# Reading the parts of a filter spectrum backwards in every second batch, under a new table of the order

## The chip, the cores and the metric

The kernel runs on one core of a Trainium2 chip. The metric is the device time of one execution in microseconds (us). Before the change three timed runs gave 484.12 us in the median (484.09 to 484.51). About 0.2%, that is 1 us, is what a measurement of this kernel can tell from no change.

## The reference

Two layers follow one another on four batches of 6272 positions with 256 channels. The first is a gated recurrence along the positions, the second a long convolution with a gate:

```python
f = lower_bound + (1 - lower_bound) * sigmoid(f_logit)      # (4, 6272, 256)
h = f[:, t] * h + (1 - f[:, t]) * x[:, t]                    # for t in 0..6271; y[:, t] = h
x1, x2, x3 = split(y @ w_proj)                               # three times 256 columns
conv = irfft(rfft(x2, axis=1) * rfft(filter_fft, axis=0))    # over all 6272 positions
out  = (x1 * conv * x3) @ w_out                              # float32
```

The spectrum of `filter_fft` doesn't depend on the batch. The kernel computes it once.

## The kernel before

**Stages.** `prepare` makes the tables and the filter's spectrum and writes the spectrum to device memory in 16 parts, `H[0]` to `H[15]` (NU = 16 units). Then each batch b goes through these steps, and the steps of neighbouring batches are interleaved:

- `hgrn(b)`: 13 chunks of 512 positions. Each loads 512 KB of `f_logit` (tile FL) and 512 KB of `x` (tile XT) from three buffers in turn, takes the sigmoid on ScalarE (L311), multiplies on GpSimd (L313), transposes on TensorE (`su`, L325), forms the gate (`f`, L338 on ScalarE or L340 on VectorE) and runs the recurrence as a scan on VectorE (L346).
- `spectrum(b)`: `phase_p` (13 groups `P`, TensorE L673, each evacuated by a copy `x2`), which needs every scan of the batch. Then, for each of four quarters, four `phase_f1` (TensorE L686, copies `A`), a small product `mini`, and four `unit`s. A unit loads its part of the spectrum into one of three slots of the tile `Hu` (NH = 3; line L721, 98 partitions of 4 KB, 392 KB in one DMA), does a transform `F2` (TensorE L731), two products with `Hu` on VectorE (`prod`, L744), and an inverse transform `I2` (TensorE L754) with its copy `Th`.
- `gate(b)`: the products of the two other projections (TensorE L373, copies `xs`, GpSimd L389).
- `phase_o(b)`: 13 groups: inverse transform `I1` (TensorE L787), product `y` on VectorE (L793), output projection `proj` (TensorE L805), a copy `o` into one of three buffers `osb` (ScalarE or VectorE, L272 and L277), and a store of 512 KB (L815). Group k's copy uses buffer k mod 3 (within batch 0), so it waits for the store of group k - 3.

**Slots.** The slot of unit u of batch b is `(16 b + u) mod 3`, and all 16 parts are loaded in each batch: 64 loads of 392 KB. A load waits until the products of the unit that had the slot before are done.

**The order.** Nothing is scheduled by a program on the chip. Every step is recorded with `op(kind, cost, fn, ...)`. `Plan.emit` then issues the steps in the order of the table `ORDER`, a string that was worked out offline. An entry of it names a step, the engine that does it and the pair of PSUM banks. Copies may be done by ScalarE or VectorE, and the table decides. Each engine works through its own entries strictly in order, and all DMAs of the kernel are issued by SyncE's one queue (SP), in order too: a DMA that waits for its buffer holds up the DMAs behind it.

In this text `o0.9` is the copy of group 9 of batch 0, `store0.6` its store, `FL3.6` the load of chunk 6 of batch 3 into FL, `P1.4` group 4 of `P` of batch 1, and `H1[u 2]` the load of the spectrum's part 2 for batch 1. A turn is the stretch around the `P` groups, where one batch gives way to the next. SP's order at the turns before the change (the steps that matter):

```
turn 0 to 1:  store0.5 FL2.1 H1[u 2] store0.6 store0.7 XT2.2 FL2.2 XT2.0 store0.8 H1[u 1] H1[u 0] H1[u 3] store0.9 H1[u 4] H1[u 5]
turn 1 to 2:  XT2.7 H2[u 1] FL2.8 ... FL3.0 H2[u 2] XT3.0 store1.7 FL3.1 FL3.2 store1.8 H2[u 0] XT3.2 H2[u 3] FL3.3 H2[u 4]
middle of 2:  store1.11 store1.10 H2[u 14] H2[u 15] XT3.6 FL3.6 H3[u 0] FL3.7 XT3.7 store1.12
turn 2 to 3:  store2.2 H3[u 1] FL3.12 store2.3 store2.5 store2.4 XT3.12 ... store2.10 H3[u 2] H3[u 3] H3[u 4] store2.8 store2.9 H3[u 5]
```

Of the kernel before, what the change touches and what calls it, by code (L numbers as in the profile page):

```python
# [25 lines left out]
TB = 98  # L26
# [32 lines left out]
class Plan:  # L59
# [58 lines left out]
    "A8gAAYBBgAOYABIAoQBLgACIBGgAmRBVgBQgAcSBagBfgAnTA7YAPIAyUBkgA9AAlVBpgBCAA+WBugBDQBAGAjSA/GBMYA6TBFABzgAgUBHY"  # L118
    "A5VBEIAQABNWERgA2SBPOA1TARIAvUBWAAYYB4gBIQAsVBRABXSADgAtUBOGBSUBYCAfWBbYESgBKAAxXArWBJABgYAeXBZCEdgBcQA3WBlA"
    "BTMBhSEpgApXBdIBqYBUEBmWATIBjCEegAUIBoGBvYBrUBeIBtEBiKAzQAFgBnGB0YBwQBsMAiSByABxIEqgB1WASAAGgAwTB5YETAB3OB9Y"  # L120
    "B6UA0SB2OAbQB7MAkRB8MCKSCIWAEYEUYCLCCBQEfACJOB/UAWICCICNSCAECEWCOKEVQCFGEgYEZUEWIAdSErAE1gAqTEXIE2gAhWEaECTS"
    "AIAAVYEbMEhWAHACDYElQAJAEsYEiOCUCCRUFBgEmAFCgEjOClSCSECQgCGgANACWUEnIE3ACMYEtWCVYCXEEuOExQE4YEvOFNgCmCCcUFOg"
    "EyACZgCaSCdMFDACjWEzIE5UCbCCkGE9SCeYE6MFEYALACfQFZgE+CE7MAuWFagAMACsWCPgAKACHgCgICuUCtGFPAFFWE/KFJQFGGFQYFjg"
    "CvEFHOCoSFkgFKAC3UChgCYgFbACpKA4WCnYFRWC4EFLIFcYCxSFSGFVUCyCFTOC1QFtgFugFWEC+SCqgEwYC2AFdWFXMCrgFlAE0YC6QCwY"
    "C5YC/CDAUC7IFmYFeGFgSDBEFfODJQFhCF3gC9gDHUDKAF4gFiKAXYFnWFvACigEcYDDQDCYFoODIEFqSFwYDEADSUFpOGBgGCgFrCDQQCzg"
    "DTEDMWC0gFsKDRADFgFMYFxUF5AC8gE8YDbQDNODLYFyEDZSDUYFAYDcADGgDVWFzMF6YDaCF0QDWGDiSF1IGLgDkUGMgDjKGDADeWEYYF2I"
    "DtSDlEDdYDYgGEYDfGDrUDOgF7QDsEDnWDuCF8IF+UDoGF9IEoYD0SGVgDmYF/EFYYD2WDqgDPgD1CDwQAaYGAMGWgD3GD/SDpgGNADxIGFW"
    "DhgDvYD5UGOYGGGEAKGIQD6EGHOD9SMVgGJADXgEIUD8gD+CEGWD4YGKIFIYEJEGPSEkYEHGGSUGXAGQKEBYECQEKYGTEMhgGYYGRKEPWD7g"
    "EDAAZYMWgMigGUMEQGGZSELQFUYGfgEFgGaCGcWJSUEEgGbKB+YGdGMXAJTVGeOJUMGgSEMAJVNGmWJWYGhCEOgDygGiUMtgMjAMugGsQDgg"
    "GnGGqSGtIDzgG0WGrCGwQHEgGjEENgGoSG1GGyUGpCGuWGzMGxAG2SGvGGkQG3KMvAG4UJXWGlAG5MJYXJcSJZGJdTJaHHLgG6QJfLG8UHSg"  # L130
    "JbYG7AJeKG+WJhTG9MG/GJgYHFQJiSJjDHHIHAWJkCJmUHBGHIIJlYJnVHMSJoEHCWJrQHPKHZgJpFJsRJtAJqYHiUJuBHOKJwQJxTJvYJyA"
    "J1RHDOHqgHjEJ2SJzLJ6QHGYJ3BHgWJ4KJ0YHJUHhGHTRHUYHKEHNYHkWJ5YHVJJ7TJ8AJ/UHlGHWJHQQJ9DHaVHRAKBMHxgJ+YHrSHcNKAX"
    "HmQHbYKCHMwYHdNHXUHnAKEXHYEHuKHeQH4gKGHIGUKDYHtKHfAHoWKFTIHEHyQHpOH/gKJSKHDH0IHsYIIUKLCKIYHvWIJEH1IH5SHzYHwG"
    "IKUH6YMYYH7KIQgH2QILEIAWH8KH3AIMUKKSINEICOIXgH9QKMCKOTIDOKPUH+AKNYKTVKQDIOQIegIRWKREIPIIBYKUSKVFKSYITOIsTKWC"
    "IEQItDIUOISYIYVIZYKXYIFAKYSIaNIlgKZUKaCKdTIuQIbNKfDKeXIvAIVSKbMI2gIfVKgHKcYIWCImQIiNKiUIcSIgYKkEKhYIhNKjXIdC"
    "KnWIpIKlHIjUI9gKpGKmYI3SIkEIoIIwWInYKoRIxGMkYI5KIqUJEgKqBKsQI6KKtWIrEI+RKvGMZUKrYJLgJAJKuAMdWMaEKxTKwYM5gMeG"
    "MbMKyQM6gKzDK2RK0AJBJIyTK4BK1YIzDMlQMfOK3VMcYMmAMpSK5FMnII0WMqCNFgMxUK6YNGgM7AI1OK7QMrKK8RI/YMyEI4YM1WM8YK+B"
    "MzMK9ANRgI7SM2GNSgLARI8CM3OLBQJGYJFULCBK/YLFSLDAJHMNHAM9WLEYNBQJIMM+GJCTNdgLHCNIYNegM/ONCALGVLKSNTANDIJMWLIF"
    "NUYJDDLLVJOONJQLMCLNFLPTJPONKANNUNfALJYNngNLINVWNogNOELQSLOYLRDNPMNZQNWGNgYRVTLSCNxgNXONaAJJUNygRXDRWSJKENbI"
    "LTYNhWRYCNkTNpANiOJNYJQQN8gNjONlDN7gNqYRaVJRARbSNmLRdCLUWRcFLZQLVONQYNrSNuUNsCLaILWWOFgNzAOGgNtKLbQNvEN0YLXG"  # L140
    "NwMLjSN9ALeWLYgLkKM0YLcAN1UN+YLfOLoSN2ELdgN4QN3MLgWN5AOPgOQgOHAMgYN6ILlULhGOIYLpKLtQLmELigN/WLuIOCSOAGLqUMsY"
    "OZgODCOBONMYOagLngNAYLyQLrEOEKNYYOJWORAOMULsgLzILvSUYgONEOSYOKGOOML0QObALwCOLOL3UMoAOcYLxgOTSM4YL4MOWWOUCL1A"
    "UkgOVKL8UPVgNEAOdQL2gOXGL9ML5SOeANcAOfIL+UL6COYOOgQL/EMGSL7gOhIUxgMBWOiIUwgMLUMCOUZgOvQMAgMHKPOgMDWOwAPHgOpS"
    "MEGOnQOqKOzWOoAO3SO0GOlQO4COtWOmAOrSOuOO5QOsCOxWO6IUyAO1SOyGMMMOjQO2CO7WMIUOkAO8OMNSUmAMJMMQQMOCO9WMRIO/UO+O"
    "RZYPBQPAEPDSPCIPIWReYPECPPUUaAPKOPFQRfSUzYRgTRhCPGIRkWRiDPLOPjQRmGPlSPkAPJYRlWRjYPSMPcgRpXRnGMFgPMQPmCPQYPRM"
    "RoYPWVRrHPdSPYNPtgPNARqUPXYRuXRsEPZNPTQRwHRtYPpUPUAPfKPnWP0gPeYPqEPaQUbYPgKPoGPuURvSP7gPbAPwMRzTUlgPrWRxCPhQ"
    "R1DPsOR0SPxMPvYP1TRyYR2CQJWPiAP4LQCgR4SQKGPyQP3LP8UR6CP9YP2YQLWPzAR3YP+MQTgP5SQMGQDQP/MP6CQNWR5UQGIQOGQagQAS"
    "R7ER9VQFIQUWQBCR8YR+RR/FQWOQhgQPSSABQEYSCUQQCSBYQHQQXOQbVQIAQRSSDXQogQdNSEESHQSFHSIRSJAQSKSGYUcUSKBQeNQvSUdE"
    "SMXQVYQwCQcYUeMQxQSLYQ5gSNWSOHQYSQyISPGQiUQZCSQYQzWQkMSRQQ0GSSRQlMQfSSUBQpWSTAQqYRAgQgCQ1USVYQsOUgQQ2ESWSQjY"
    "QrOU9gUnYUhASXTQmUSZDUiIRHgSYCQtWU8gQnEQ3SQ6QSaYQ4KQuGRBUQ8ISbSRCYScTSdCSgWRDMSeDShXSiGUoSSfYREMSjHSlQUpCSmU"  # L150
    "SkYQ9ISnASqWSoESrXQ7YRIUU+AUqKSpYROgQ+QMPgSsGStPU/YRFSQ/ARLMUsWRGCSvQVIgRKMUtGRPRVJgSxASuYSwVUuOS0TSyFS1QRJY"
    "S2DSzYU0URSJS3AS5WU1ES6XRQYRRJS4YS7GU4SS8HS+QVUgU2MS9YVKARTWVVgS/RRUGU5KRMUVLYTBJTAATDWRNEU6KVAQTEXVBATFOVEU"
    "TCYTGHVCITISVFEVhgVMWVggTHYVWAVGMMKgVQQTJTVNGVqgVXYTKKMSUTLDVOOVRATNSMTETOTTPCMUgTSUVSITMYTQDVYVVrgXRgTTXVZF"
    "TXSTRYTVPTUEVcQVaNViATWYZYXV0gZZUV1gVdAVjYZdVTYKZeWZaHZgGZfNTZSVsAVeITcWTaCTdOThQVtYZbEVkSTbgVnUTiIVlCTeWV+g"
    "VoEV/gVmKVuQTfGVpMTmSV2ATggVxWTnKWJgTjUVvAV3YWIgVyGVwITrSTkEVzOWAATlgV4QV7UV5ATsKWBYToWWSgUjAV8EV6ITtSTpGV9M"
    "T1QUvYTuCTqgTwWVPYWTgUfAT2IWCSTvgU3YVbAWFUU7YWDCTxOT3QWcgWKAWdgWEKTyWWGEWLYWUAWHMT6STzGT7KT/UVTYT4AWMWUAMWPS"
    "WVYWNGT5gT8QWQCT0gWOOUEUT9AWRKVHYWWWWeAVfYWZQWXGUFMWfYUBScogWaAVDYcbgUrAWYOXYgUGUUCCccgT+gWbIWgWWjScngWhGUHE"
    "czgWiOUDgUJQWkKUOWWlKUKIW+UXKgW4SW/EUPOW0Qc0gW5CULUW1AW8WcdAWoSW9OWyQWpCWsWUMEWwSWtOWzAW2UcpAWuQW3EcqYW6WWvA"
    "WmUW7OWxCWqQWnMUQWWrAUTSURGXAUUUKXCQZhYXBMXESXDAXGWZcYXFKXLUXHGXSQceYc1AXOMXISZiWZjXZkGXJKZnVZlHXVIXmSZpFXMY"
    "XoWXnCZmYZoVXNMZsRZqFcfSXTYZuBXUIZrYXfgcjUcgCZtRc/gXpGchKZxQXwgdAgckEZyWZvJcrSZzAclMZ0GXWQcsCZ1YXsWXXActKXgU"  # L160
    "ZwYXZQXtGXjMcvSXhYdBAXPWc2YXiMZ2VcwCXQGXcIZ3UX+gdLgZ4FXqWUIgcxKZ5EZ7RXrGZ8VZ6YaAUXbIaBSZ9BXkWXaYaDCZ+NX3gaCE"
    "XdQdMgXlGZ/YXuSX4UXvKXeAYOWX5YXxSdCYYPGYMQX0Kc3WYNAXzKaFTc4GaEYc7QaHDX6MYFgaGSc8AaKTaICX7MaLUaMDaJYaPSaNEaQT"
    "c9IdNAYWgX8UXyYdYgaOYdXgX9EaSLX1Qc5OaRCdOYX/TX2AaUVYBLaVSaWFYQWaXCYGQYCLaTYYRGYSSaZVYIIYTCYdgaYYaaWaeXabFafU"
    "YJIYHYacGdDSYAYc6YahEYUVajQdECYkgYVNadYakRagHdFKYKUdZAYDWYfYaiYamJalAYXSYEGaoRYZKanYYLEYyWapQYzGYaKYeUYYYatS"
    "arAYgMYbWYrgaqBavCY0QasYYhMYcGYlTauSY1AYmYYoLYiWY8gawCY2QYjGYtYYnLaxYYsUY3AaySYuMY4WZDgdaYa0CYpQUSgY5GUNgYvM"
# [21 lines left out]
def kernel(  # L187
# [102 lines left out]
    def halves(pb, hn):  # L290

        a = PS[:, pb, 0:hn]
        return bass.AP(tensor=a.tensor, offset=a.offset,
                       ap=[a.ap[0], [768, 2], a.ap[1]])

    count = dict(x=0, f=0, s=0, o=0)


    def hgrn(b):
        for c in range(NCHK):  # L300
            t0 = c * CH
            nb = min(CH, S - t0) // 128
# [574 lines left out]
```

## Time and profile before

| | before |
|---|---|
| median of three timed runs | 484.12 us |
| the profiled execution's own time | 487.22 us |
| its span | 485.2 us |
| TensorE (PE) busy, share of the span | 451.7 us, 93% |
| VectorE (DVE) busy | 413.3 us, 85% |
| ScalarE (ACT) busy | 423.0 us, 87% |
| GpSimd (POOL) busy | 299.6 us, 62% |
| moved by DMA | 116.49 MB, 240 GB/s in the mean |
| share of the 16 DMA engines taken by the kernel's queue | 70.0% |

The profiled execution took 2.0 us more than its span, and 3.1 us more than the median of the timed runs. In the rows, a time is that of the profiled execution, counted from the span's start. PE is TensorE's matmuls, PEld its weight loads; SPq is the queue of SyncE. "idle before" with an arrow names the work whose end released the waiting instruction. The chain of waits follows the execution back from its last instruction, always to what came last. Tables by stretch give the busy time of each engine in a stretch with the number of its instructions, then the granted TensorE clock as a share of full speed, the mean busy share of the DMA engines, and GB/s moved.

### The profile page before, as it was taken

To read this page: it belongs to the slowest core of one execution; us is meant where nothing else is said; L and a number is where in the kernel's file an instruction comes from. 1 tells how busy PE (TensorE), PEld (TensorE's weight loads), DVE (VectorE), ACT (ScalarE), POOL (GpSimd) and SP (SyncE) were. 2 spreads that over 40 slices of the span, in tenths; PEclk is the share of its full clock that TensorE was granted. 3 is DMA by queue.
4 is the path that set the end of the run, shared out by engine and by line. 5 is a ranking of instruction groups with operands and counts; after the bars stand their busy time and mean duration, and the time that the engine had idled before them with its cause. 6 is when DMAs were issued, how large, how long until landed. Compare 5 with 4: busy or idle time off the path is not lost.

```text
span 485.2 us, 14710 instructions
## 1 busy us (share of the span) xinstructions
PE 451.7 (93%) x6041; PEld 347.1 (72%) x6041; DVE 413.3 (85%) x446; ACT 423.0 (87%) x613; POOL 299.6 (62%) x313
## 2 busy tenths in 40 slices
PE   8988998999999989999998998989989899999995
PEld 7776777677667879767566888656757788676784
DVE  7788985899999985999999984979989984999773
ACT  6988999999998969989898978999979868999844
POOL 6775994486897910946896723878675522666600
PEclk9999999999999999999999999999999999999998
DMA  8989999545688994464879975475777861544177
GB/s 330 397 287 354 329 306 313 188 122 162 208 274 291 356 346 173 134 195 135 240 236 360 386 265 228 152 232 190 227 245 250 315 227 38 178 148 151 54 287 294
DMA packets 41731, 116.49 MB, mean 240 GB/s; under 512 B 4384, under 2 KB 6304, under 8 KB 41664
## 3 DMA queue, kind: packets, MB, share of 16 engines
q1 hardware_dynamic: 41664, 115.56, 70.0%
q8 instruction: 47, 0.77, 0.7%
q14 instruction: 20, 0.16, 0.1%
HBM read 84.54 MB, written 31.00 MB: 238 GB/s over the span
## 4 chain that ended last, share of the span: by engine, by line
PE 46%; DMA 17%; DVE 14%; ACT 10%; issue 5%; POOL 3%; SPq 1%; ACTq 0%; DVEq 0%; POOLq 0%
PE PS L373 11%; DMA out_dram<-osb 8%; PE PS L673 7%; DMA FL<-in_f_logit_dram 6%; PE PS L754 6%; DVE PP L744 5%; PE PS L805 5%; DVE HA L346 5%; PE PS L731 4%; PE PS L686 4%; PE PS L325 4%; DMA Hu<-H 2%; ACT osb L272 2%; ACT fTs L338 2%; PE PS L787 2%
## 5 line engine op out<-in xcount | busy, mean ns | idle before, releaser
L389 POOL TENSOR_TENSOR zt<-x1s,x3s 128x490 f16<-128x490 f32 (+1 forms) x104 | 125.3, 1214 | 94.5 <-ACT x3s L270 43.9
L744 DVE TENSOR_TENSOR PP<-PS,Hu 98x1008 f16<-98x1008 f32 x128 | 146.5, 1199 | 8.6 <-PE PS L731 3.3
L313 POOL TENSOR_TENSOR XT<-XT,FL 128x1024 f32<-128x1024 f32 (+1 forms) x52 | 116.8, 2247 | 47.5 <-ACT FL L311 18.6
L346 DVE TENSOR_TENSOR_SCAN HA<-fTs,HA,PS 128x512 f16<-128x512 f32 (+1 forms) x96 | 113.4, 1204 | 6.9 <-ACT fTs L338 5.9
L373 PE MATMUL PS<-HA,W 128*128 128x490 f16 (+1 forms) x416 | 105.5, 370 | 3.1 <-DVE PP L744 1.4
L793 DVE TENSOR_TENSOR ys<-PS,zt 128x1024 fp32r<-128x1024 f32 (+1 forms) x52 | 58.6, 1151 | 9.0 <-PE PS L787 3.6
L272 ACT ACTIVATE osb<-PS 128x1024 f32<-128x1024 f32 (+1 forms) x49 | 47.7, 988 | 19.6 <-PE PS L805 11.1
L338 ACT ACTIVATE fTs<-PS,nomc 128x512 f32<-128x512 f32 (+1 forms) x89 | 59.3, 680 | 4.6 <-PE PS L325 4.1
L270 ACT CAST HA<-PS 128x1024 f16<-128x1024 f32 x57 | 57.8, 1032 | 3.8 <-PE PS L686 3.3
L805 PE MATMUL PS<-Wo,ys 128*128 128x256 f32 x392 | 56.8, 291 | 3.2 <-ACT osb L272 1.7
L311 ACT ACTIVATE FL<-FL 128x1024 f32<-128x1024 f32 (+1 forms) x52 | 53.1, 1021 | 7.6 <-DMA FL<-in_f_logit_dram 7.4
L272 ACT ACTIVATE x1s<-PS 128x490 f32<-128x490 f32 (+1 forms) x95 | 56.0, 592 | 3.5 <-PE PS L373 1.3
L373 PEld LDWEIGHTS <-W 128*128 128x128 f16 x416 | 33.9, 98 | 33.7 <-issue 10.8
L754 PEld LDWEIGHTS <-PP 98*128 98x128 f16 x1024 | 49.5, 98 | 11.9 <-issue 3.3
L270 ACT COPY x3s<-PS 128x490 f32<-128x490 f32 (+1 forms) x90 | 51.8, 579 | 4.6 <-PE PS L373 3.1
L805 PEld LDWEIGHTS PS<-Wo,ys 128*128 128x128 f32 x392 | 49.0, 188 | 7.9 <-ACT osb L272 2.2
L325 PE MATMUL PS<-iden,FL 64*128 64x64 f32 x784 | 46.6, 233 | 7.8 <-ACT afs L270 2.1
L754 PE MATMUL PS<-VA,PP 98*128 98x98 f16 x512 | 51.8, 207 | 1.6 <-DVE HA L346 0.9
L270 ACT CAST Th<-PS 128x784 f16<-128x784 f32 x62 | 50.9, 830 | 1.4 <-PE PS L754 1.2
L325 PEld LDWEIGHTS PS<-iden,FL 64*128 64x128 f32 x784 | 34.0, 139 | 25.2 <-DVE HA L346 5.6
L754 PE MATMUL PS<-VB,PP 98*128 98x98 f16 x512 | 51.6, 207 | 0.0
L673 PE MATMUL PS<-W,HA 128*128 128x256 f16 x392 | 44.8, 273 | 3.4 <-ACT osb L272 3.4
(110 smaller groups left out, 677.9 us busy)
## 6 DMA issues: line engine op xcount, KB each, us to landing
Hu<-H SPq DMA_DIRECT2D x64, 392.0 KB
FL<-in_f_logit_dram SPq DMA_DIRECT2D x48, 512.0 KB
XT<-in_x_dram SPq DMA_DIRECT2D x48, 512.0 KB
out_dram<-osb SPq DMA_DIRECT2D x48, 512.0 KB
X<-in_moe_filter_fft_dram SPq DMA_DIRECT2D x9, 512.0 KB
H<-Hu SPq DMA_DIRECT2D x16, 196.0 KB
H<-Hu SPq DMA_DIRECT2D x16, 128.0 KB
Hu<-in_moe_filter_fft_dram SPq DMA_DIRECT2D x2, 512.0 KB
```

The source lines that it names most:

```text
L270: nc.scalar.copy(dst, src)
L272: nc.scalar.activation(dst, src, AF.Copy, scale=scale)
L313: op("u", {"POOL": 0.1 + 0.553 * nb}, lambda e, xt=xt, ft=ft: nc.gpsimd.tensor_tensor(xt, xt, ft, op=AOP.mult), r=[("ft", k)], w=[("xt", k)])
L325: nc.tensor.transpose(bank(pb)[:, at[p] + j:at[p] + hn:nb], src[ps, j, cols], iden[ps, ps])
L338: nc.scalar.activation(fT, sT, AF.Identity, scale=by, bias=1.0)
L346: nc.vector.tensor_tensor_scan(h, fT, bank(pb)[:, 512 - hn:512 + hn], init, op0=AOP.mult, op1=AOP.add),
L373: nc.tensor.matmul(PS[:, p, 0:n], W13[:, kh, js], HA[:, HB[kh] + t0:HB[kh] + t0 + n], start=(kh == 0), stop=(kh == 1))
L389: nc.gpsimd.tensor_tensor(late["zt"][:, jb, :, m0:m0 + nm], xs(0), xs(1), op=AOP.mult),
L673: nc.tensor.matmul(pp[:, r - r0, :], column(HB[kh], q_of(r)), W2[:, kh, :], start=(kh == 0), stop=(kh == 1))
L744: nc.vector.tensor_tensor(PP[:TB, k, o, :, :, 1:64], px.unsqueeze(1).broadcast_to([TB, 2, UE, 63]), hh[:, :, :, 1:64], op=AOP.mult)
L754: nc.tensor.matmul(PS[:, ib + o, pr * TB:(pr + 1) * TB], PP[:TB, k, o, n, 2 * pr:2 * pr + 2, :], v[:TB], start=(n == 0), stop=(n == 1))
L805: nc.tensor.matmul(po[:, i, :], late["ys"][:, yk, kh, i * 128:(i + 1) * 128], Wo[:, kh, :], start=(kh == 0), stop=(kh == 1))
```

## The change

`unit` no longer computes its slot from the batch and the unit. The list `held` says which part lies in each of the three slots, and `recent` orders the slots by their last use. A unit whose part is held takes that slot and issues no load; any other takes the slot that has gone unused longest. In batches 1 and 3 the quarters, and the units in each, are taken from the last to the first. Batch 0 ends on parts 13, 14 and 15, and batch 1 begins with 15, 14, 13; it ends on 2, 1, 0, with which batch 2 begins; and so on. So the first three units of batches 1, 2 and 3 have no load, and 55 of the 64 loads remain.

```diff
+    held, recent = [None] * NH, list(range(NH))
+
+    def spectrum_load(u, h):
+        first = count["h"] < NH
+        count["h"] += 1
+        held[h] = u
+        op("H", {"SP": 0.46}, lambda e: nc.sync.dma_start(
+            Hu[:TB, h].rearrange("p a e k -> p a (e k)"), twice(H[u][:])),
...
     def unit(b, u):
         ka = u % NA * UE
-        k = (b * NU + u) % NP
-        h = (b * NU + u) % NH
-        op("H", {"SP": 0.46}, lambda e: nc.sync.dma_start(
...
+        k = count["u"] % NP
+        count["u"] += 1
+        h = held.index(u) if u in held else recent[0]
+        recent.remove(h)
+        recent.append(h)
+        if held[h] != u:
+            spectrum_load(u, h)
...
     def spectrum(b):
         phase_p(b)
-        for q in range(NU // NA):
-            for u in range(q * NA, q * NA + NA):
+        way = 1 if b % 2 == 0 else -1
+        for q in range(NU // NA)[::way]:
+            for u in range(q * NA, q * NA + NA)[::way]:
                 phase_f1(b, u)
             mini(b, q)
-            for u in range(q * NA, q * NA + NA):
+            for u in range(q * NA, q * NA + NA)[::way]:
                 unit(b, u)
```

The string `ORDER` is replaced as a whole. From the two built programs, engine by engine:

- TensorE has the same 770 steps. Up to a few neighbours that change places they stand in the same order, but for the turns. At turn 0 to 1 the old table has one `P` group, `proj0.9`, then the other twelve; the new one has ten `P` groups, `proj0.9`, two, `I1` 11 and 12, the last. At turn 1 to 2 the old one has `proj1.10` after three `P` groups and `proj1.11` after all, the new one has both after all thirteen.
- 11 more steps are done by VectorE (406 for 395), 7 fewer by ScalarE, 4 fewer by GpSimd. VectorE's part of the copies changes thus: `x2` +4, `afs` +4, `f` +3, `o` +3, `Th` +1, `fr` +1, `f2` -3, `hw` -2. Four of GpSimd's `wrap` copies (L280) go to ScalarE. `o0.9`, `o1.10` and `o2.10`, done by ScalarE before, are done by VectorE at the turns, `o0.9` after ten `P` groups and `o1.10` after all thirteen; `o0.12` goes to VectorE in the middle of batch 1, `o1.12` leaves it.
- SP's order at the same places:

```
turn 0 to 1:  store0.5 FL2.1 XT2.1 store0.6 store0.8 XT2.2 XT2.0 FL2.2 store0.7 H1[u 12] H1[u 11] ... H1[u 5] store0.11 H1[u 4] store0.10 H1[u 3] H1[u 2] H1[u 1] FL2.3 XT2.3 store0.9 H1[u 0]
turn 1 to 2:  XT2.7 XT2.8 ... store1.5 store1.6 store1.7 FL3.0 store1.8 FL3.1 FL3.2 XT3.0 XT3.2 XT3.1 store1.9 H2[u 3] XT3.3 H2[u 4] FL3.3
middle of 2:  store1.10 H2[u 11] ... H2[u 15] FL3.6 store1.11 XT3.6 XT3.7 FL3.7
turn 2 to 3:  store2.2 store2.3 FL3.12 XT3.12 store2.4 store2.5 store2.6 store2.7 store2.10 store2.8 H3[u 12] H3[u 11] ... H3[u 5] store2.9 H3[u 4]
```

- In `prepare`, the loads of `x` for batch 1 (XT1.0, XT1.1) come after the last stores of the spectrum and the first two loads of it, where before they came ahead of them; two fewer of the spectrum's stores stand ahead of XT0.11 (14 for 16).

## The prediction

> **What bounds the kernel now.** I read the page first (busy shares and the DMA row), then the table in stretches of 10 us, then the chain of waits and the order of time at the turns.
>
> ```profile
> PE 451.7 (93%) x6041; PEld 347.1 (72%) x6041; DVE 413.3 (85%) x446; ACT 423.0 (87%) x613; POOL 299.6 (62%) x313
> ...
> DMA  8989999545688994464879975475777861544177
> ...
> Hu<-H SPq DMA_DIRECT2D x64, 392.0 KB
> ```
>
> No engine is the bound throughout. TensorE is idle for 485.2 - 451.7 = 33.5 us, and no more than that, plus a lower clock, can be won at its waits. The DMA row is full in four places: up to 90 us, and around the three turns. There the table shows who pays:
>
> ```profile
> 160.00:170.00 10.00, 10.00 (x162) 8.87 (x158) 10.00 (x10) 9.28 (x13) 8.88 (x8) 1.00 1.01 349
> 170.00:180.00 10.00, 9.37 (x157) 8.33 (x152) 8.95 (x10) 7.22 (x11) 1.49 (x3) 1.00 0.99 331
> 180.00:190.00 10.00, 8.26 (x77) 8.13 (x76) 4.15 (x4) 7.42 (x8) 0.00 (x0) 1.00 0.80 291
> ...
> 290.00:300.00 10.00, 8.35 (x75) 8.13 (x74) 4.50 (x4) 7.96 (x9) 2.40 (x1) 1.00 0.81 320
> ```
>
> The columns after the stretch are PE, PEld, DVE, ACT, POOL, clock, DMA share and GB/s. At 160 to 180 the DMA share is 1.0 at 331 to 349 GB/s, and TensorE's idle time comes directly after. The order of time names the wait:
>
> ```profile
> 171.87 0.65 SPq L721 DMA_DIRECT2D Hu<-H  x1
> 172.72 3.13 SPq L815 DMA_DIRECT2D out_dram<-osb  x2
> ...
> 181.71 1.02 ACT L272 ACTIVATE osb<-PS 128x1024 f32<-128x1024 f32 x1 [2.38 <-DMA out_dram<-osb]
> ```
>
> `store0.6` goes out directly behind a load of the spectrum that nobody needs before 196 us. In the chain of waits it takes 8.89 us to land; ScalarE holds `o0.9` for it, and with it everything behind; the next `P` group waits for that copy's PSUM pair, 1.74 us of TensorE. Turn 1 to 2 repeats it: a load of the spectrum at 283.68, `store1.7` at 284.58, which lands after 9.19 us, `o1.10` at 293.79, TensorE idle for 1.65 us before 294.87.
>
> **The change part by part.** *The nine loads.* Each is 392 KB, that is 0.401 MB, and at the mean of the two rows, 340 GB/s, takes 1.18 us of a full queue: 3.5 us at each turn, 10.6 us in all. [...] But eight of the nine were issued in full stretches (171.87, two from 179.27, 253.75, 283.68, 287.81, 352.84, 378.46; only 398.53 is not), and what they push back are stores and loads that are waited for. So the gain isn't 10.6 us but what TensorE gets back of its waits there:
>
> - (a) Turn 0 to 1: 1.74 us. `store0.6` loses the load ahead of it (1.2 us), and `o0.9` now comes after ten `P` groups on VectorE, some 8 us later (the chain has 8.24 us for 74 of a batch's 98 `P` matmuls, 0.11 us each, and eight in a group), when the store has landed. I take 1.7; ends 0 and 1.7.
> - (b) Turn 1 to 2: the same for `o1.10` and `store1.7`, 1.65 us; the stretch 260 to 280 has 2.0 us more of idle TensorE, scattered over waits for FL, XT and `osb`; one load (253.75) goes from ahead of it. I take 1.6 + 0.4 = 2.0; ends 0 and 3.7.
> - (c) Middle of batch 2. `FL3.6` is issued at 350.46 behind two loads of the spectrum, two stores and XT3.6, and lands after 9.12 us. TensorE then has 1.9 us idle in 354 to 362, and after it a lower clock:
>
> ```profile
> 362.00:364.00 2.00, 2.00 (x30) 1.25 (x30) 1.16 (x2) 1.63 (x3) 2.00 (x2) 0.56 0.09 30
> 364.00:366.00 2.00, 2.00 (x16) 1.00 (x12) 1.60 (x2) 1.23 (x3) 0.15 (x2) 0.59 0.40 86
> ```
>
>   Four us at 0.575 cost up to 1.7 us. [...] In the new order `FL3.6` has neither XT3.6 nor the stores 1.10 and 1.11 directly ahead, and all of batch 2's loads of the spectrum. I take 1.5; ends 0 and 3.6.
> - (d) Before turn 2 to 3, 378 to 396, TensorE lacks 2.9 us in small waits for `osb` stores, FL and scans. The load at 378.46 stands ahead of FL3.12 and `store2.3`. One load's time: 1.2; ends 0 and 2.9.
> - (e) In batch 1, the load issued at 201.19 lands 5.85 us later, and VectorE's product is 1.54 us late for it. Between it and the load before, `store0.9` went out; that store now comes after eleven loads more. TensorE has about 1 us of gaps after it. I take 0.5; ends 0 and 1.5.
>
> *The order in `prepare`.* XT0.11, issued at 62.01, is on the chain for 7.12 us. It loses two spectrum stores ahead (0.16 MB each, together 1 us of queue). Everything else up to 77 us is the same work shuffled. I take 0.5; ends -1.5 and 1.5.
>
> *The copies that change engine.* By the rows (x2 1.24, afs 0.68, f 0.66, o 1.25, Th 0.97, fr about 1.05, f2 0.64, hw 1.21 us on VectorE), +4, +4, +3, +3, +1, +1, -3, -2 make 11.1 us more for VectorE, 424 in all. Of this the four `x2` and three of the `o` (8.7 us) lie at the turns, where VectorE is busy 4 to 5 of 10 us: nothing, as long as TensorE's `P` groups (10.9 us in a row) cover it; without that cover, up to 8.7. The other 2.4 us are spread over stretches where VectorE is at 9 to 10 of 10: I take 0.6 lost; ends 0 and 2.4. The four `wrap` copies cost ScalarE 4 x 0.63 us, less than it hands over.
>
> *Waits.* No step is added. Three `o` that waited for stores on ScalarE now do so on VectorE, with `y`, the copies `A` and the first products behind them; that is the rival below. No load passes another queue, since all DMAs are SP's; its 309 ns per issue are free.
>
> Sum: 1.7 + 2.0 + 1.5 + 1.2 + 0.5 + 0.5 - 0.6 = 6.8 us. Not all of it stays. From 130 to 170 VectorE is busy 9.85 to 10 of 10 us, and from 200 to 280 9.3 and more in most slices; a stage that starts earlier meets these sooner, and some waits form again. I keep 70% (my choice): 4.8 us. The profiled execution should go from 487.2 to about 482.4, its span from 485.2 to 480.4; the timed runs, 3.1 us below it, from 484.1 to 479.3.
>
> **Rivals.** *The transfers were hidden, and the table's shuffling gives back the rest.* For it: GpSimd, not on the path, is what waits longest for DMAs, and the DMA row is below 1 in 27 of 40 slices. Against: the two waits at the turns end in idle TensorE. It keeps the 1.7 us of (a) at most and loses 1.5 in `prepare`: 484.1 - 0.2, about 483.9.
>
> *Slower: a store holds VectorE at the turn.* In the new order `store0.7` goes out after `store0.8` and three loads of 512 KB, two of which wait for buffers; `o0.10` needs it, on VectorE, ahead of the copies `A1.0`, `A1.2` and all products of batch 1. Before, the loads were out at 177.5, so the store goes at 178 and, with the turn's 8.9 us, lands at 187; `o0.10` came at 192.1, or 190.3 with (a). The slack is 3.3 us; it decides against the change if the stores land more than 12 us after issue. Then (a) becomes a wait in another place, and if the same happens to `o1.10` (one of the last steps before `A2.0`), two waits of some 3 us take the place of the gains of (a) and (b): 484.1 + 6 - 0.7 x (1.5 + 1.2 + 0.5 + 0.5) = 487.5. Against it: 1.2 MB less is in the queue, and DMA share falls to 0.03 at 190 to 200, so the queue was empty before `o0.10`.
>
> *More than I count.* All ends (a) to (d) come in: 1.7 + 3.7 + 3.6 + 2.9 = 11.9, of which 70% are 8.3: 475.8.
>
> *That the change doesn't do what it says* can be ruled out: 55 loads stand in the program's order.
>
> **How the numbers follow.** Forecast 479.3 (its own range 477 to 482.5): 0.58. More than I count, 475.8: 0.14. Hidden, 483.9: 0.13, of which 0.03 below 483.15. Slower, 487.5: 0.15. A measurement tells 0.2%, 1 us, from no change. Faster than 483.15: 0.58 + 0.14 + 0.03 = 0.75; within: 0.10; above 485.1: 0.15. The range 475.0 to 485.1 leaves out the slower case and the far half of the larger gain.
>
> **What would show it.** 55 loads of `Hu`, 3.6 MB less. (a), (b): no wait of `P` for an `osb` copy at the turns, and 13 `P` groups in a row; if VectorE's `o0.10` waits for DMA, the rival is right. (c): no clock below 1.00 near 360, FL3.6 landing in under 7 us. (e): no product late for a load in batch 1's first half. `P` of batch 0 should start at 77 rather than 77.5. I am wrong if the DMA rows at the turns stay at 1.0 for as long, or if a new low-clock stretch opens elsewhere.

## The result and the profile after

| | before | after |
|---|---|---|
| median of the runs | 484.11 us (482.25 to 484.51, four runs) | 476.47 us (475.14 to 478.41, four runs) |
| ratio, after to before | | 0.9853, 95% interval 0.981 to 0.9895 |
| the profiled execution's own time | 487.22 us | 478.41 us |
| its span | 485.2 us | 476.4 us |

The change makes the kernel faster by 1.5%; by the interval the gain is 5.1 to 9.2 us. The timed runs differ by 7.6 us and the profiled executions by 8.8. The forecast was 479.3, so the gain was 2.8 us larger than forecast; the range and the sign held. (The profiled execution of the last experiment was a slow one; its profile isn't read, only its times are.)

After the change the lines below the load stand lower: the load of the spectrum is L723, `I1` L802, `y` L808, `proj` L820, the store L830; `P` (L673) and the copies (L272, L277) keep theirs. From the page of the kernel after:

```profile
PE 447.8 (94%) x6041; PEld 345.4 (72%) x6041; DVE 424.9 (89%) x457; ACT 416.1 (87%) x606; POOL 297.9 (63%) x309
...
DMA  8989998636588897157769995567588831356277
...
Hu<-H SPq DMA_DIRECT2D x55, 392.0 KB
```

VectorE has the 424 us that the prediction worked out for it, the loads are 55, and TensorE is idle for 476.4 - 447.8 = 28.6 us where it was idle for 33.5. The DMA row is about as full around the turns as it was. The table by stretch, with its columns as before, is where the change shows:

```profile
160.00:170.00 10.00, 9.46 (x162) 8.20 (x161) 9.77 (x10) 9.31 (x14) 5.09 (x4) 1.00 0.94 338
170.00:180.00 10.00, 9.11 (x147) 8.20 (x146) 9.86 (x11) 8.68 (x13) 4.10 (x5) 1.00 0.96 321
180.00:190.00 10.00, 10.00 (x106) 9.68 (x104) 5.49 (x6) 8.56 (x10) 0.00 (x0) 1.00 0.82 280
...
290.00:300.00 10.00, 9.92 (x110) 8.46 (x109) 8.20 (x9) 8.27 (x10) 7.08 (x4) 1.00 0.29 113
```

At 180 to 190 TensorE had 8.26 us of work and a queue at 0.80; now it has 10.00, and the queue is at 0.82. From 160 to 190 the DMA share is 0.94, 0.96 and 0.82 where it was 1.01, 0.99 and 0.80. So the queue hardly got emptier, which comes close to what the prediction had named as a sign of being wrong; what changed is that TensorE no longer depends on it. The chain of waits (start, duration, what) says how it goes through the turn:

```profile
178.33 8.89 PE PS L673 x80
187.22 0.94 PE PS L820 x8
188.16 1.16 PE PS L673 x10
```

The 8.89 us of a store's landing that stood here are gone from the chain, and ten of the `P` groups (80 matmuls) run in one piece. The store itself is no faster. `store0.6` is the first of these two stores, and `o0.9`, which needs its buffer, is this copy on VectorE:

```profile
174.16 5.02 SPq L830 DMA_DIRECT2D out_dram<-osb  x2
```

```profile
188.26 1.22 DVE L277 TENSOR_SCALAR osb<-PS 128x1024 f32<-128x1024 f32 x1 [0.58 <-PE PS L820]
```

The store is down at 183.23, 9.07 us after its issue, and five us before the copy that needs it. (Where no copy waits for a transfer, I read its landing in the trace from its semaphore: the sixteen rises of that of `store0.6` run from 179.93 to 183.23.) The low clock near 364 is gone too:

```profile
362.00:364.00 2.00, 1.82 (x36) 1.61 (x37) 1.69 (x3) 2.00 (x4) 2.00 (x1) 1.00 0.43 168
364.00:366.00 2.00, 1.98 (x43) 1.67 (x43) 2.00 (x2) 1.63 (x3) 0.14 (x1) 1.00 0.99 330
```

Another wait now stands on the chain right behind that place, with its cost in the table by stretch:

```profile
366.38 8.92 DMA FL<-in_f_logit_dram
```

```profile
370.00:380.00 10.00, 7.90 (x152) 6.92 (x146) 8.52 (x8) 7.32 (x10) 5.59 (x4) 1.00 0.84 332
```

A load of `f_logit` for batch 3 lands 8.92 us after its issue, and TensorE is idle for 2.10 us of these ten. Before, the same work stood nearly ten us later, at 380 to 390, with 7.74 us of TensorE and so 2.26 us idle: this loss was not won back.

To see where the 8.8 us of the span come from, I took from both traces the start of the first matmul of each stage, to 0.1 us: the first `P`, `F1` and `I1` of each batch.

| stretch | before, us | after, us | gain |
|---|---|---|---|
| up to the first `P` of batch 0 | 77.3 | 78.7 | -1.4 |
| batch 0, `P` to `I1` | 75.2 | 74.9 | 0.3 |
| turn 0 to 1 (`I1` of batch 0 to `F1` of batch 1) | 40.6 | 39.1 | 1.5 |
| batch 1, `F1` to `I1` | 61.0 | 59.8 | 1.2 |
| turn 1 to 2 | 46.6 | 42.9 | 3.7 |
| batch 2, `F1` to `I1` | 65.6 | 61.6 | 4.0 |
| turn 2 to 3 | 43.7 | 43.4 | 0.3 |
| batch 3, `F1` to the end | 75.2 | 76.0 | -0.8 |

### The profile page after: what moved, and what is told of

Read it like the earlier page. It is cut to its first block, busy times and chain, and to the rows that moved or that the text cites. A ratio compares the mean times of both kernels' runs of the same rounds, so it can differ in the third digit from the quotient of the medians.

```text
span 476.4 us, 14713 instructions
## 1 busy us (share of the span) xinstructions
PE 447.8 (94%) x6041; PEld 345.4 (72%) x6041; DVE 424.9 (89%) x457; ACT 416.1 (87%) x606; POOL 297.9 (63%) x309
## 4 chain that ended last, share of the span: by engine, by line
PE 52%; DVE 16%; DMA 12%; POOL 6%; ACT 6%; issue 6%; SPq 0%; ACTq 0%; DVEq 0%; POOLq 0%
PE PS L373 13%; PE PS L673 9%; DVE HA L346 8%; PE PS L768 8%; PE PS L745 6%; PE PS L686 5%; DVE ys L808 5%; PE PS L325 4%; DMA XT<-in_x_dram 4%; DMA X<-in_moe_filter_fft_dram 4%; PE PS L820 3%; POOL zt L389 3%; POOL XT L313 3%; DMA out_dram<-osb 2%; DVE PP L758 2%
## 5 line engine op out<-in xcount | busy, mean ns | idle before, releaser
L808 DVE TENSOR_TENSOR ys<-PS,zt 128x1024 fp32r<-128x1024 f32 (+1 forms) x52 | 58.8, 1150 | 8.5 <-PE PS L802 6.5
L820 PE MATMUL PS<-Wo,ys 128*128 128x256 f32 x392 | 57.8, 293 | 3.5 <-DVE ys L808 2.5
L338 ACT ACTIVATE fTs<-PS,nomc 128x512 f32<-128x512 f32 (+1 forms) x86 | 56.2, 672 | 4.8 <-PE PS L325 4.3
L272 ACT ACTIVATE osb<-PS 128x1024 f32<-128x1024 f32 (+1 forms) x46 | 45.0, 985 | 16.9 <-DMA out_dram<-osb 8.7
L270 ACT COPY x3s<-PS 128x490 f32<-128x490 f32 (+1 forms) x96 | 54.6, 574 | 4.0 <-PE PS L373 1.8
L820 PEld LDWEIGHTS PS<-Wo,ys 128*128 128x128 f32 x392 | 49.3, 188 | 9.0 <-DVE ys L808 4.6
L272 ACT ACTIVATE x1s<-PS 128x490 f32<-128x490 f32 (+1 forms) x89 | 52.1, 592 | 3.9 <-PE PS L373 2.2
L673 PE MATMUL PS<-W,HA 128*128 128x256 f16 x392 | 44.6, 274 | 0.2 <-DVE HA L346 0.2
```

Of the source, the lines that this page charges most:

```text
L270: nc.scalar.copy(dst, src)
L272: nc.scalar.activation(dst, src, AF.Copy, scale=scale)
L673: nc.tensor.matmul(pp[:, r - r0, :], column(HB[kh], q_of(r)), W2[:, kh, :], start=(kh == 0), stop=(kh == 1))
L808: nc.vector.tensor_tensor(late["ys"][:, yk, :, 0:rn * 128], PS[:, cb:cb + 2, 0:rn * 128], late["zt"][:].rearrange("p k r m -> p k (r m)") ...
L820: nc.tensor.matmul(po[:, i, :], late["ys"][:, yk, kh, i * 128:(i + 1) * 128], Wo[:, kh, :], start=(kh == 0), stop=(kh == 1))
```

## The experiments

The change has two parts, and they can be had apart: the nine loads that go, and the new table. The prediction rested on the first (call it theory Q: the loads made room in the queue). The rival is R: the table alone would have done it. Twelve kernels were run. The table lists all; the last four columns are the stretches of the table above, from one profiled execution of each. The turn 1 to 2 shows how far single profiles can be trusted: before and "FL3.6 first" have the same order up to its end, and take 46.6 and 44.8 us.

| kernel | loads of H | ratio to before, 95% interval | median us | turn 0-1 | turn 1-2 | batch 2 | turn 2-3 |
|---|---|---|---|---|---|---|---|
| before | 64 | 1 | 484.1 | 40.6 | 46.6 | 65.6 | 43.7 |
| after | 55 | 0.9853 (0.981, 0.9895) | 476.47 | 39.1 | 42.9 | 61.6 | 43.4 |
| new table, loads back | 64 | 0.9825 (0.9788, 0.9862) | 476.53 | 39.3 | 42.8 | 61.6 | 42.5 |
| old table, loads out | 55 | 0.9945 (0.9915, 0.9975) | 481.86 | 39.6 | 44.8 | 63.2 | 42.7 |
| old `prepare`, rest new (first) | 55 | 0.9887 (0.9844, 0.993) | 479.98 | 39.5 | 43.7 | 61.6 | 43.2 |
| old table, FL3.6 first | 64 | 0.9971 (0.9936, 1.0006) | 482.55 | 40.4 | 44.8 | 62.5 | 43.4 |
| old `prepare`, rest new (second) | 55 | 0.9858 (0.98, 0.9916) | 477.6 | 39.0 | 43.1 | 61.8 | 43.0 |
| new table, old turns, loads back | 64 | 0.9986 (0.9955, 1.0018) | 483.1 | 42.4 | 43.4 | 62.6 | 43.2 |
| new table, old turns | 55 | 0.9968 (0.9935, 1.0) | 482.01 | 42.2 | 43.4 | 62.7 | 42.0 |
| new table, FL3.6 last | 55 | 0.985 (0.9804, 0.9896) | 476.74 | 39.8 | 42.9 | 61.6 | 43.0 |
| new table, old first turn | 55 | 0.9882 (0.9835, 0.9928) | 479.5 | 41.6 | 43.1 | 61.6 | 42.8 |
| new table, old second and third turn | 55 | 0.9895 (0.9846, 0.9944) | 479.74 | 39.2 | 44.5 | 62.7 | 43.1 |
| new table, `o0.9` early | 55 | 0.9884 (0.9837, 0.9931) | 479.53 | 41.3 | 44.5 | 61.6 | 42.7 |
| old table, a few steps moved (meant: new turns) | 64 | 1.0003 (0.9971, 1.0035) | 485.07 | | | | |

The last four ran on a chip on which the kernel before took 486.4 us in the median, so ratios are compared and not medians. A ratio of 0.99 is 4.8 us below 484.1.

### The loads and the table apart

New table with the loads back: the rule of the slots is the changed one, but the first three units of batches 1 to 3 load again; in SP's order each such load stands about where the old table had it, the first of them directly ahead of `store0.6` again.

```diff
-        if held[h] != u:
+        if held[h] != u or plan.batch > 0 and count["u"] % NU in (1, 2, 3):
```

> The changed kernel and its table, with the nine loads put back: the first three units of batches 1, 2 and 3 load again what their slot already holds, at the places in the DMA queue where these loads stood before (64 loads again, the rest of the order untouched). Theory Q (the gain comes from 3.6 MB less in the full stretches): the larger part of the 7.6 us is lost again, 480 to 482 us. Rival R (the gain comes from what the new table moves, the loads were hidden): at most 1 us is lost, 476 to 477.5.

Measured: 0.9825, which isn't slower than the changed kernel (0.9853 lies in its interval), and 8.5 us below before. Q falls as the cause of the whole: in the new table the nine loads cost nothing that can be told. (The two intervals together leave room for a cost of some 1.4 us, by my estimate.) The profile shows that they are not free for want of load on the queue. From SP's timeline at the first turn (start, duration, engine, line):

```profile
175.96 0.37 SPq L723 DMA_DIRECT2D Hu<-H  x1
176.42 4.56 SPq L830 DMA_DIRECT2D out_dram<-osb  x2
```

and from the table by stretch:

```profile
180.00:190.00 10.00, 9.86 (x90) 9.87 (x91) 6.07 (x6) 8.03 (x9) 0.00 (x0) 1.00 0.97 349
```

The load stands directly ahead of a store as it did before, the queue is at 0.97 and 349 GB/s, fuller than before (0.80, 291), and TensorE has 9.86 of 10 us.

Old table with the loads out: the changed unit with the old `ORDER`, the nine steps taken out of it.

> The other half alone: odd batches backwards and the nine loads gone, but every other step in the order, on the engine and in the PSUM banks of the table of before (unit u of an odd batch stands where unit 15 - u stood). Q: 479 to 480.5, most of the gain. R: 483.5 to 484.5, no gain. If neither half alone gives much, the two only work together: the stores' waits at the turns need both.

Measured: 0.9945, 2.7 us below before, interval 1.2 to 4.1. That is between the two expectations: the loads' absence is worth something under the old table. Its chain at the first turn has no store in it:

```profile
177.53 1.03 PE PS L673 x8
178.56 0.94 PE PS L820 x8
179.50 9.89 PE PS L673 x90
```

`store0.6`, issued at 173.04, is down at 178.59, and `o0.9` runs on ScalarE at 179.59 and doesn't wait. So the prediction's term (a) happens there as it was argued: take the load out from ahead of `store0.6`, and the wait goes. But the new table takes the same wait away without that, and the two don't add up: alone they gain 2.7 and 8.5 us, together 7.1.

### `prepare`, and the place of FL3.6

Old `prepare` with the rest new was built twice. In the first build, at the seam, where the two orders meet, a PSUM bank is written again before the copy of the spectrum's last part has read it, so that this part's values are others; the second build has the seam further on (ahead of the first `F1`) and no such overlap. The amount of work is the same in both.

> The changed kernel with the steps of prepare and of the first recurrence in the order of before (their engines and banks too), everything after them as in the new table. In the profiles, the new table's first P group of batch 0 starts 1.3 us later (78.7 for 77.3). If the order makes that and it reaches the end: 475.2, 1.3 below the changed kernel. If the stage's length is the transfers' alone, or the 1.3 us are taken up later: 476.5, as the changed kernel.

> All steps up to the first forward unit of batch 0 stand in the old table's order; everything after that, and the 55 loads, as in the changed kernel. In the profiles so far the first P of batch 0 starts at 78.7 and 79.1 us with the new order of the preparation, and at 76.3, 77.0 and 77.3 us with the old one. If those 2 us belong to the order of the preparation and reach the end, this kernel takes 474.5 to 475 us, below the changed kernel's 476.5. If they are spread between executions, or are made up for later, it takes 476 to 477 us.

Measured: 0.9887 and 0.9858. The second is as good as the changed kernel's 0.9853. In its profile the first `P` starts at 79.7 us, with the old order of `prepare`, the latest of those read; with the same order it started at 76.3 us with the old table and the loads out. With the new order it started at 76.8 us (old first turn) to 79.1 us (loads back). So this start differs by 2 to 3 us between executions under either order, and the 1.4 us by which it was later after the change can't be put down to the change. (Up to 1.7 us of the 79.7 are a half clock at 42.1, of the kind shown below.)

The load FL3.6 was tested from both sides: brought ahead of the two stores and of XT3.6 in the old table, and put behind `store1.11` and XT3.6 in the new one.

```diff
-middle of 2, old table:  store1.11 store1.10 H2[u 14] H2[u 15] XT3.6 FL3.6 H3[u 0]
+                         FL3.6 ahead of these
-middle of 2, new table:  H2[u 11] ... H2[u 15] FL3.6 store1.11 XT3.6 XT3.7
+                         H2[u 11] ... H2[u 15] store1.11 XT3.6 FL3.6 XT3.7
```

> The kernel before with one move in the DMA queue: in the middle of batch 2, FL3.6 goes out directly behind the loads of parts 14 and 15, and the stores 1.11 and 1.10 and XT3.6 come behind it; all 64 loads, nothing else. It tests term (c), the largest difference between the two traces (4 us between the first F1 and the first I1 of batch 2). If that stall and the low clock after it come from what stood ahead of FL3.6: 1.5 to 3.5 us faster than before, 481 to 482.5. If the timed runs don't have the stall (it may be the profiled execution's own, which is 3.1 us above the median), or XT3.6 behind FL3.6 is waited for as long: 484.

> The changed kernel with one thing undone in SyncE's queue: the load FL3.6 goes out behind the store 1.11 and the load XT3.6, as before the change. If term (c) is that place in the queue, the stretch from the first forward to the first inverse unit of batch 2 grows from 61.6 us towards 65.6 and the time to 478 to 480.5 us. If the load was late before for the transfers of the whole batch and not for its place, 476 to 477 us.

Measured: 0.9971 with an interval up to 1.0006, so nothing that can be told from before, though batch 2's stretch is 62.5 us in its profile; and 0.985, with the stretch at 61.6, so nothing lost by putting it back. In the new table the place of FL3.6 is not what batch 2 gains. And at 350 to 368 the low clock stands in the profile of before alone: the clock there is 1.00 in the seven others that I read, the old table with the loads out among them. But it isn't peculiar to before. A half clock for 3.41 us also stands in the profiles of the new table with the loads back (147.3), the second old `prepare` (42.1), the old second and third turn (31.5) and `o0.9` early (146.0). From the first of these:

```profile
143.90:147.30 3.40, 2.00 (x48) 1.73 (x46) 3.40 (x4) 3.22 (x6) 3.40 (x4) 1.00 0.70 199
147.30:150.70 3.40, 3.40 (x30) 1.84 (x29) 2.95 (x3) 2.77 (x6) 3.40 (x3) 0.50 0.81 265
```

The mean clock was 0.992 to 0.995 in these five executions and 0.996 to 0.999 in the other eight that were profiled and read. In all five, TensorE was busy for only 1.50 to 2.10 us of the 3.4 to 3.5 us before (in before, 1.99 of 3.4 from 358.8). Such a stretch isn't always followed by one: before has 1.91 of 3.4 us busy from 181.3 and after has 2.00 from 372.5, both with a full clock behind them. So the low clock did follow a late load in before (FL3.6, 9.12 us), as the prediction read it, but it stands in five profiles of thirteen, at five different places, and what sets it off isn't shown. By my estimate, half of 3.41 us, it costs up to 1.7 us; so it can also explain why batch 0 takes 1.2 us longer in the profiles with the loads back and with `o0.9` early.

### The turns

The next kernels have the old table's order from the last two sums of a batch to the first `F1` of the next, and the new one in all the rest; at the seams some PSUM pairs had to be swapped for free ones. At the first turn this is the change on TensorE and ScalarE:

```diff
-P1.4 P1.6 P1.2 P1.11 P1.8 P1.1 P1.0 P1.7 P1.3 P1.9 proj0.9 P1.12 P1.5 I1[11] I1[12] P1.10 proj0.10 proj0.11
+P1.6 proj0.9 P1.3 P1.2 P1.8 P1.10 P1.1 P1.5 P1.4 P1.11 P1.7 P1.9 P1.0 P1.12 proj0.10 proj0.11 I1[12]
-ScalarE: o0.8 x2 x2 x2 ...          VectorE: y0.9 x2 x2 x2 o0.9 ...
+ScalarE: o0.8 x2 o0.9 x2 x2 ...     VectorE: y0.9 y0.10 x2 x2 x2 ...
```

> The new table with all 64 loads of H, but at the three turns (from sum 24 of a batch to its first forward unit) the old table's order. Theory T, that the order of the new table at the turns is what makes the nine loads free: the waits of terms (a) and (b) return, so 479 to 480 us, with the stretch from the last inverse of a batch to the first forward unit of the next 1.5 to 3.5 us longer at the first two turns. Rival M, that the gain comes from the middle of the batches and the turns' order is indifferent: 476 to 477 us.

> The same with the nine loads left out: new table in the middle of the batches, old order at the turns, 55 loads. If taking the load out from ahead of the store is as good at the turns as the new order, 476.5 to 477.5 us. If the turns need the new order, 479 to 480 us. Together with the run that has the loads back, it says whether order and removal stand in for each other: then only the kernel with old turns and all loads is slow.

Measured: 0.9986 and 0.9968. Of the 8.5 us (loads back) 0.7 are left and of the 7.1 (loads out) 1.5, so more is lost than theory T said, and the loads make no difference that can be told. In the profiles the first turn takes 42.4 and 42.2 us, longer than before. The kernel without the loads shows that the wait has come back; first its table by stretch, then its chain:

```profile
180.00:190.00 10.00, 8.98 (x82) 8.80 (x81) 3.96 (x4) 7.29 (x8) 0.00 (x0) 1.00 0.62 251
```

```profile
173.04 9.36 DMA out_dram<-osb
...
182.51 1.03 ACT osb L272
183.54 0.04 issue
183.59 3.67 PE PS L673 x32
```

A store out at 173.04 lands at 182.40, after 9.36 us, with no load of the spectrum near it. The old table with the loads out issues the same stores at the same 173.04, and there the first was down at 178.59, after 5.55 us. SP's timelines tell the two apart. Old table, loads out:

```profile
171.70 0.34 SPq L308 DMA_DIRECT2D FL<-in_f_logit_dram  x1
173.04 3.12 SPq L830 DMA_DIRECT2D out_dram<-osb  x2
```

New table, old turns, loads out:

```profile
172.13 0.34 SPq L308 DMA_DIRECT2D FL<-in_f_logit_dram  x1
172.58 0.37 SPq L308 DMA_DIRECT2D XT<-in_x_dram  x1
173.04 3.17 SPq L830 DMA_DIRECT2D out_dram<-osb  x2
```

The new table has brought XT2.1 (512 KB) to where the 392 KB of the spectrum had been. I take this to be why removal does nothing for the old turn in the new table: another transfer has taken the place. XT2.1 alone wasn't moved to test it, and the landings fit it only loosely. In the twelve profiles with a transfer directly ahead of `store0.6`, the store takes 6.49 us (`o0.9` early) to 9.36 us, and the old table alone, with the same load ahead, gives 8.89 and 7.33; the 5.55 us without one are a single execution.

One turn at a time:

> The changed kernel with the old table's order at the first turn alone (from sum 24 of batch 0's successor to the first forward unit of batch 1), 55 loads. With all three turns in the old order and no loads the time was 482.0 us, 5.5 above the changed kernel, and in its profile the stretch from the last inverse unit of batch 0 to the first forward unit of batch 1 was 42.2 us against 39.1. Theory F, that the first turn carries most of it: 479 to 481 us, with that stretch at 41.5 us or more. Rival S, that the loss is spread over the turns: 478 us or below.

> The old order at the second and the third turn alone, 55 loads. Theory F: 476.5 to 478.5 us, since the first turn has the new order. Rival S: 479 to 480.5 us. The two losses should add up to about the 5.5 us of the run with all three turns old; if they don't, the turns act on each other.

Measured: 0.9882 and 0.9895, 1.4 and 2.0 us above the changed kernel by the ratios, but the intervals overlap with its own, so each by itself isn't told from it in time; neither F nor S has won. Their sum, 3.4 of the 5.6 us that all three old turns cost, isn't told from the whole either. The profiles put it thus: with the old first turn, that turn takes 41.6 us (2.5 more), and no other stretch of the table differs by over 0.6; with the other two old, batches 2 and 3 take 1.1 and 1.0 us more between `F1` and `I1`. Turn 1 to 2 takes 1.6 more there, but that isn't the order's: the next kernel has the new order at this turn and the same 44.5 us. In both a load of `f_logit` ahead of the turn lands late (7.79 and 8.74 us on their chains). The chain of the first of them has the wait again:

```profile
172.38 8.69 DMA out_dram<-osb
...
181.17 1.03 ACT osb L272
182.20 0.04 issue
182.25 3.67 PE PS L673 x32
```

Then the smallest edit, one block's end in the changed kernel:

```diff
-TensorE: P1.4 P1.6 P1.2 P1.11 ... P1.9 proj0.9 P1.12
+TensorE: P1.4 P1.6 proj0.9 P1.2 P1.11 ... P1.9 P1.12
-VectorE: y0.10 y0.9 x2 x2 x2 o0.9        ScalarE: o0.8 x2 x2 x2
+VectorE: y0.9 y0.10 x2 x2 x2             ScalarE: o0.8 x2 x2 o0.9 x2
```

> The changed kernel with one block's end moved back: y0.9, projection 0.9 and copy o0.9 stand where the old table had them, the projection behind two of batch 1's P and the copy on ScalarE behind two of its copies, in place of behind ten of them and on VectorE. The copy needs the buffer that store 0.6 empties, and that store took 9.4 us to land in the run with old turns and no loads, until 182.4 us. Theory O, that this one wait is what the first turn loses: 478.5 to 480.5 us, and ScalarE's copies waiting 1.5 us or more for a store ahead of a P. Rival: with the rest of the turn in the new order the wait is short or has cover, and the time is 476 to 477.5 us.

Measured: 0.9884, that is 1.5 us above the changed kernel, with an interval that takes in its 0.9853. The turn takes 41.3 us, where it takes 39.0 to 39.8 in the six profiles read with this turn in the new order. The size is about as theory O said, the wait is not. From the chain:

```profile
179.02 2.33 DVE ys L808 x2
...
181.40 1.22 PE PS L820 x8
...
182.69 1.02 ACT osb L272
183.71 0.91 ACT X L270
184.62 0.04 issue
184.67 2.79 PE PS L673 x24
```

No store is waited for: `store0.6` is down at 181.46, after 6.49 us. Here `proj0.9` waits for `y0.9`; ScalarE is idle for 0.54 us until `proj0.9` is done, does the copy of 1.02 us, and only then goes on with the copies of `P`, for which TensorE waits. It waits for another thing than before, with the same effect. So the cost goes with the place of this block's end: a copy that waits for something, ahead of the copies that keep `P` going. By the new table it comes after ten groups, on VectorE, and nothing of `P` is behind it but three groups. Place and engine were moved together, so which of the two counts isn't shown.

Last, the reverse was meant: the old table and all 64 loads, with the new order at the three turns only.

> The kernel before with all of its 64 loads and its table, but with the new table's order at the three turns. If the turns carry the whole of the gain, 476 to 478 us. If the middle of the batches gives as much as the turns do and either repairs the other, also below 478 us. If the gain needs both, 480 us or more.

Measured: 1.0003 (0.9971 to 1.0035), no gain at all. But the table that ran doesn't hold the new turns. Read step by step, TensorE and VectorE have exactly the old table's order (one `P` group, `proj0.9`, then the other twelve), and `o0.9` and `o1.10` are still on ScalarE. All that moved is three transfers, two sigmoids and two products on GpSimd:

```diff
-SP, old table:  H1[u 6] XT2.1 H1[u 7]     FL3.4 store1.9 H2[u 5]    H3[u 4] store2.8 store2.9
+SP, this run:   H1[u 2] XT2.1 store0.6    XT3.2 store1.9 H2[u 3]    H3[u 2] store2.8 H3[u 3]
```

So it says that moving these few steps is worth nothing, and nothing about the new turns in the old table; that kernel was never run. What the record has is one side: with all loads in, the new middle without the new turns gives 0.7 us, and with them 8.5. The new turns carry nearly all of the gain there. Whether they would also carry it without the new middle is open.

## Why the prediction was right, and for which wrong reason

The number, the sign and the range held; the attribution did not, and that the terms still came near the number is in part luck, as (b) and (c) were too low and (d) and `prepare` too high. The prediction made the nine loads the source: "the gain isn't 10.6 us but what TensorE gets back of its waits there". The waits did go, but in the changed kernel they go because of the table, and they go with all 64 loads in.

- **(a) Turn 0 to 1, 1.7.** Measured 1.5, and TensorE's 1.74 us at 180 to 190 came back in full. The prediction gave two reasons at once, the load gone and `o0.9` ten groups later. Each is enough by itself in one of the runs: the first under the old table, the second with the loads back. They must not be counted as cause and help; and in the changed kernel the first is no cause at all, as `store0.6` takes 9.07 us to land, no less than the 8.89 before.
- **(b) Turn 1 to 2, 2.0.** Measured 3.7, the upper end; up to 1.8 of it may be the profile of before, as "FL3.6 first" takes 44.8 us with the same order. Its reason, the load ahead of `store1.7`, failed: without it the old table takes 44.8 us too, and with old turns and all loads in the new table the turn takes 43.4 us, with that load again directly ahead of that store. The timeline and then the chain of that kernel:

```profile
279.78 0.41 SPq L724 DMA_DIRECT2D Hu<-H  x1
280.76 0.33 SPq L831 DMA_DIRECT2D out_dram<-osb  x1
```

```profile
288.36 8.80 PE PS L674 x80
```

  (its lines are one lower). The store goes out at 280.76, 4.5 us ahead of the first `P`, and is down after 5.13 us. Before, it went at 284.58, 0.9 us ahead, and took 9.19. It was late because FL3.0 ahead of it got its buffer from GpSimd at 281.96 only and took SP until 283.58; in the new middle FL3.0, XT3.0 and XT3.1 stand behind the store. The step that failed put the wait down to the one load of the spectrum, where three other loads stood ahead as well; that these are the cause is my reading, not tested alone.
- **(c) Middle of batch 2, 1.5.** Measured 4.0, above the upper end of 3.6 (1.9 us of idle time and 1.7 of low clock). The place of FL3.6 was the stated reason. FL3.6 does land in 5.0 us now, under the 7 that were asked for, but moving it back costs nothing. Up to 1.7 us of the 4.0 are, by the same estimate, the low clock, which stands in five of the thirteen profiles and at this place in that of before alone; the loads out under the old table, FL3.6 first under the old table, and the new middle with old turns each brought the stretch to 62.5 to 63.2 us. I can't name one cause for the rest.
- **(d) Before turn 2 to 3, 1.2.** Measured 0.3. The load of the spectrum ahead of FL3.12 is gone, and TensorE still loses 2.1 us in the same work, where it lost 2.3 before. Then a store (8.48 us from 378.02) was on the chain there, now it is a load of `f_logit` (8.92 us from 366.38): one wait has turned into another.
- **(e) Batch 1 and `prepare`.** 0.5 and 0.5 forecast, 1.2 and -1.4 measured. The second differs between executions by more than either number. No product in batch 1's first half is idle for a load any more: the longest such wait there, 0.82 us, is for `F2`.
- **VectorE, -0.6.** The 11.1 us more are there to 0.5 us (11.6). What they cost can't be read apart: batch 3 takes 0.8 us longer, batch 0 0.3 less.
- **The 70%.** The terms made 6.8, the parts measured 8.8 in the profile and 7.6 in the runs. The discount stood for waits that form again; that is seen in (d) alone, and (b) and (c) were sized too low besides. Without it the forecast would have been 477.3.

**The rivals.** *Slower, a store holds VectorE*: no copy on VectorE waits for a store at the first turn; its waits of 0.9 us there are for TensorE's `proj`, and in the whole execution one copy on VectorE waits for a store, for 0.7 us. *Hidden* was right in one half: the nine transfers are hidden in the changed kernel, where the loads back give 0.9825 and the loads out 0.9853. It was wrong that the table then gives nothing. And under the old table the same loads cost 2.7 us (1.2 to 4.1). I read this as depending on who waits for what is queued behind the transfer. The 10.6 us of full queue are the prediction's estimate from the two rows' 340 GB/s; no run here measures them.

Three places in the prediction's text were wrong in detail, with no weight in its sum: the DMA row is under 9 in 31 of 40 slices (not 27); `store0.9` comes after twelve of batch 1's thirteen loads; and in the new middle of batch 2 `store1.10` and the last loads of the spectrum still stand ahead of FL3.6, only `store1.11` and XT3.6 have gone behind it.

**What is shown and what is open.** Shown: the nine loads are worth nothing that can be told in the new table and 2.7 us in the old; in the new table, the old order at the turns loses most of the gain; at the first turn it goes with the place of `o0.9` and what feeds it, in the length of the turn. Open: what the new turns give in the old table, whether the place or the engine of `o0.9` counts, and the single causes at turn 1 to 2 and in batch 2. All spliced kernels also have seams that no planner saw, which may cost something of their own; the second `prepare` splice and the two moves of FL3.6 show that a seam or a move need not.

## What to carry to other kernels

Before you credit a removed transfer with a wait, put it back under the new order: here 8.5 us stayed. In a kernel whose engines each follow a fixed list, ask of every copy that waits for a transfer what is queued behind it on its engine; moved behind ten groups that don't need it, the copy no longer held them up, though the transfer took as long as before (9.07 us for 8.89). And read the table of a spliced kernel step by step before you draw on its time: one of twelve here wasn't what it was meant to be.

## What was not expected of the hardware

- One store of 512 KB in the full queue (DMA share 0.89 to 0.99 at 170 to 180, in eight profiles), `store0.6`, took 6.49 to 9.36 us to land in twelve profiles with another transfer directly ahead of it, and 5.55 us in the one without. Two executions with the same order up to there gave 8.89 and 7.33.
- Executions of one kernel on one chip differ by more than the effects that were looked for: before took 481.9 to 487.8 us in 23 runs, at a mean clock of 0.991 to 1.000. The 1 us that the text ahead of the prediction takes as told from no change is too small: a gain of 1.4 us, as of FL3.6 first, wasn't told from nothing with 12 runs.
- Part of this spread goes with the clock: the higher mean clock goes with the shorter time (correlation -0.35 in these 23 runs, -0.49 in 23 others on this chip, -0.61 in 16 on the other). A half clock for 3.41 us costs up to 1.7 us by my estimate, half of its length, and lies in the midst of five of the thirteen profiles read, at five different places.
